# One batch at a time in a cached-attention decode block: V in 64 KB rows, K in two halves, one softmax per batch

## The chip, the cores and the metric

One core of one Trainium2 chip runs one launch. Times are microseconds of device time. A time quoted for a kernel is the median of its runs. For a core that runs alone, a run counts as slow when it lies more than 1.5% above the fastest of the same kernel; comparisons use the fast runs, and a kernel seen only once has no state ("unknown"). All ratios below are the mean time of one kernel's fast runs over that of the other's fast runs of the same rounds (the profiled run left out), so they are not quite the ratio of the medians that I quote.

## The reference, cut to what matters

A decode step for eight sequences. Each has one new token, 32 query heads of 128, four kv heads, and a cache of 8192 positions.

```python
q = (h @ wq).reshape(8, 1, 32, 128)                      # h: modulated layernorm of x
scores = einsum('bhqd,bhkd->bhqk', q, k) * 128 ** -0.5   # k, v: 8 query heads share a kv head
o = einsum('bhqk,bhkd->bhqd', softmax(scores), v)
x = x + ga * (o @ wo)
gate, up = h2 @ W_gate, h2 @ W_up                        # h2: modulated layernorm of the new x
x = x + gb * ((gate * (gate > 0) * up) @ W_down)
```

K and V are 16.8 MB per batch together, 134 MB of the 186 MB that the program reads. Every byte is used once, so the bytes set a floor.

## The kernel before: the parts that matter

The kernel works on a half batch m at a time (two kv heads, 64 partitions each). K and V arrive in four rotating slots of 32 KB a partition. K is transposed by the vector engine (DVE) in eight pieces; the tensor engine (PE) multiplies each with Q; a max per row, spread over partitions by a small matmul, gives the exponential's bias; the probabilities are transposed by DVE; PE multiplies them with V. The result of P·V is folded by DVE at the next half batch.

```python
for m in range(M):                                  # M = 16 half batches
    for nm, t in (("k", A_k_cache), ("v", A_v_cache)):
        load((nm, m), ...rearrange("g (p c) d -> (g p) (c d)", p=64), 2 * SLOT)   # 32 KB a partition
...
for m in range(M):
    P.trip = m // 2                                 # two half batches per turn of the hardware loop
    for e8 in range(8):
        kt_part(m, e8); qk_part(m, e8)              # DVE transpose, then four matmuls
        if e8 == 5: rowmax(m, 0)
    fold(m - 1, 0); fold(m - 1, 1)
    rowmax(m, 1); spread(m)
    fold(m - 1, 2); headmax(m); expo(m); fold(m - 1, 3)
    fold_pe(m - 1); keep(m - 1)
    p_turn(m)
    make_qpad(m + 2)
    pv(m)
```

A helper turns the list of operations into a loop with counted semaphores. For each instruction of a turn it works out how far a counter must have come. This part is the same in both kernels; remember the expression `need[t][at] - base[sem] - t * by`, where `need` is 0 when an instruction waits for nothing.

```python
base[sem] = last[0] - by          # what the counter stands at when the first turn begins
for at in range(len(trips[0])):   # each instruction of a turn
    v = max(need[t][at] - base[sem] - t * by for t in range(n))
    if v > top:
        limit[at][sem] = top = v  # this instruction waits for the counter to reach v
```

Of the kernel before, what the change touches and what calls it, by code (L numbers as in the profile page):

```python
# [6 lines left out]
dt = mybir.dt  # L7
ACT = mybir.ActivationFunctionType
# [255 lines left out]
def bass_adaLN_cond__gqa_block_cached__glu_gated_reglu__decode_kernel(nc, A_x, A_k_cache, A_v_cache, A_wq, A_wo, B_x, B_W_gate, B_W_up, B_W_down, c, w_mod, out):  # L264
# [11 lines left out]
    SLOT = 8192  # L276
    RING = 16 * 4096
# [13 lines left out]
    with ExitStack() as es:  # L291
# [9 lines left out]
        ktb = sb("kt", [128, NKT * 2048], dt.bfloat16)  # L301
# [5 lines left out]
        jm = sb("jm", [128, 2, J], dt.float32)  # L307
        jms = sb("jms", [128, 2 * J], dt.float32)
        jmp = sb("jmp", [128, 2, J], dt.float32)
        im = sb("im", [128, 4], dt.float32)  # L310
# [10 lines left out]
        M = N // 2  # L321
        qR = sb("qR", [128, 4, M, J], dt.bfloat16)
        rq = sb("rq", [128, 2, 128], dt.bfloat16)
        mq = sb("mq", [128, 4], dt.bfloat16)
        qpad = sb("qpad", [128, 2, 4, 152], dt.bfloat16)
        prb = sb("prb", [128, 1024], dt.bfloat16)
        pT = sb("pT", [128, 2, 32, 2, 32], dt.bfloat16)
        negm = sb("negm", [128, 4], dt.float32)
        mj = sb("mj", [128, 2 * J], dt.float32)
        mjt = sb("mjt", [128, 2 * J], dt.float32)  # L330
        bias = sb("bias", [128, 2], dt.float32)
        lall = sb("lall", [128, M], dt.float32)
        lx = sb("lx", [128, M, 2 * J], dt.float32)
        om = sb("om", [128, Dh], dt.float32)
        oacc = sb("oacc", [128, M + 1, 2 * J], dt.float32)
# [21 lines left out]
        for t in "kv":  # L357
            for i in range(2):
                sems[(t, i)] = E(nc.semaphore("%s_%d" % (t, i)))

        def at(m):

            return m if P.turn is None else 2 * P.turn + m % 2
# [12 lines left out]
        stream, place, cursor = [], {}, [0]  # L376

        def load(key, src, n):
            stream.append((key, src, n))

        def pump():
            while stream:
                key, src, n = stream[0]
                lo = cursor[0] if cursor[0] + n <= RING else 0
                if P.unread("arena", lo, lo + n):
                    return
                stream.pop(0)
                cursor[0] = lo + n
                place[key] = lo
                dst = arena[:, lo:lo + n]  # L390
                if len(src.shape) == 3:
                    dst = dst.rearrange("p (a n) -> p a n", a=src.shape[1])
                P.op("sp", lambda e, dst=dst, src=src: e.dma_start(dst, src), writes=[slot_r(lo, lo + n)], dma=True,
                     own=(key[0], key[1] % 2) if key[0] in "kv" else None)
                if key[0] in "kv":
                    P.held[key] = (lo, lo + n)
# [7 lines left out]
        load(("wm", 0), wm_src[:, 0:D], D)  # L404
        load(("wm0", 0), wm_src[:, D:24 * D], 23 * D)
        load(("wm", 1), wm_src[:, 24 * D:48 * D], 24 * D)
        for i in range(2):
            load(("wq", i), wq_src[:, 2 * i * SLOT:2 * (i + 1) * SLOT], 2 * SLOT)
        for m in range(M):
            for nm, t in (("k", A_k_cache), ("v", A_v_cache)):  # L410
                load((nm, m), t[m // 2, 2 * (m % 2):2 * (m % 2) + 2].rearrange("g (p c) d -> (g p) (c d)", p=64), 2 * SLOT)
        wo_parts = [(0, 16), (16, 32)]
        for i, (r0, r1) in enumerate(wo_parts):
            load(("wo", i), wo_src[:, r0 * D:r1 * D], (r1 - r0) * D)
        gu_parts = [(0, 4), (4, 8)]
        for i, (r0, r1) in enumerate(gu_parts):
            load(("gate", i), g_src[:, r0 * F:r1 * F], (r1 - r0) * F)
            load(("up", i), u_src[:, r0 * F:r1 * F], (r1 - r0) * F)
        wd_parts = [(0, 14), (14, 21), (21, 25), (25, 27), (27, 28)]
        for i, (r0, r1) in enumerate(wd_parts):  # L420
            load(("wd", i), d_src[:, r0 * D:r1 * D], (r1 - r0) * D)
# [10 lines left out]
        def aff(e, t, base, pat):  # L432
# [9 lines left out]
        P.op("pool", lambda e: e.memset(qpad[:], 0.0), writes=[R("qpad", 0, 2)])  # L442
        P.op("pool", lambda e: e.memset(pT[:], 0.0), writes=[R("pT", 0, 4)])
# [6 lines left out]
        P.op("pool", lambda e: e.tensor_copy(rq[:].rearrange("p t (h l x) -> p (t h) l x", h=2, l=2),  # L450
                                             identf[:].rearrange("p (q x) -> p q x", q=4)[:, :, None, :].to_broadcast([128, 4, 2, 32])),
             reads=[R("identf")], writes=[R("rq")])

# [21 lines left out]
        P.op("dve", lambda e: e.tensor_reduce(jm[:], identf[:].rearrange("p (g m j) -> p g j m", g=2, j=J), AX.X, ALU.add),  # L475
             reads=[R("identf")], writes=[R("jm")])
        P.op("dve", lambda e: e.tensor_reduce(jmp[:], identf[:].rearrange("p (t g i j) -> p g j t i", t=2, g=2, j=J), AX.XY,
                                              ALU.add), reads=[R("identf")], writes=[R("jmp")])
        P.op("dve", lambda e: e.tensor_reduce(im[:], identf[:].rearrange("p (t i j) -> p i t j", t=4, j=J), AX.XY, ALU.add),
# [58 lines left out]
        for i in range(2):  # L538
            fns = []
            for kk in range(4 * i, 4 * i + 4):  # L540
                w = arena[:, place["wq", i] + (kk % 4) * 4096:place["wq", i] + (kk % 4 + 1) * 4096].rearrange("p (g z n) -> p g z n", g=4, z=2)
                for z in range(2):
                    for g in range(4):
                        fns.append(lambda e, w=w, z=z, g=g, kk=kk: hold(e.matmul(  # L544
                            ps[32 * g:32 * g + 32, 3 + z, :], hT[:, kk, :], w[:, g, z, :],
                            start=(kk == 0), stop=(kk == KC - 1), tile_position=(0, 32 * g)), z > 0))
            P.op("pe", fns, reads=[R("hT"), slot_r(place["wq", i], place["wq", i] + 2 * SLOT)], writes=[bank(3, 2)])
        qs = ktb[:, 6144:7168].rearrange("p (i x) -> p i x", x=32)
        qT = ktb[:, 7168:8192].rearrange("p (i r) -> p i r", r=32)
        for z in range(2):  # L550
            src = ps[:, 3 + z, :].rearrange("p (u x r) -> p u r x", u=J, r=2)
            dst = qs[:, 16 * z:16 * z + 16, :].rearrange("p (u r) x -> p u r x", r=2)
            res, resT = ("kt", 6144 + 512 * z, 6656 + 512 * z), ("kt", 7168 + 512 * z, 7680 + 512 * z)
            if z == 0:
                P.op("dve", lambda e, s=src, d=dst: e.tensor_copy(d, s), reads=[bank(3 + z)], writes=[res])  # L555
            else:
                P.op("act", lambda e, s=src, d=dst: e.activation(d, s, ACT.Copy), reads=[bank(3 + z)], writes=[res])
# [5 lines left out]
        P.op("pe", [lambda e, t=t: e.matmul(ps[:, 5, 256 * t:256 * t + 256].rearrange("p (i b) -> p i b", b=B), rq[:, t, :],  # L563
                                            qT[:, :, 0:2 * B:2], start=True, stop=True) for t in range(2)],
             reads=[("kt", 7168, 8192), R("rq")], writes=[bank(5)])
        for u in range(4):
            src = ps[:, 5, :].rearrange("p (t j u b) -> p u b t j", t=2, j=J, u=4)[:, u]
            P.op("dve", lambda e, s=src, u=u: e.tensor_copy(qR[:, u].rearrange("p (b t) j -> p b t j", t=2), s),
                 reads=[bank(5)], writes=[R("qR", u, u + 1)])



        QE = SLOT // 4

        def make_qpad(m):
            if m >= M:
                return
            P.op("pool", lambda e: e.tensor_tensor(  # L578
                out=qpad[:, m % 2, :, 24:152].rearrange("p u (q c) -> p u q c", q=4)[:, :, :, 0:J],
                in0=qR[:, :, m, None, :].to_broadcast([128, 4, 4, J]), in1=mq[:, None, :, None].to_broadcast([128, 4, 4, J]),  # L580
                op=ALU.mult), reads=[R("qR", 0, 4), R("mq")], writes=[R("qpad", m % 2, m % 2 + 1)])

        def kt_part(m, e8):
            lo = place["k", m] + e8 * QE
            to = (8 * m + e8) % NKT * QE
            P.op("dve", lambda e: e.transpose(ktb[:, to:to + QE].bitcast(dt.uint32), arena[:, lo:lo + QE].bitcast(dt.uint32)),  # L586
                 reads=[slot_r(lo, lo + QE)], writes=[R("kt", to, to + QE)], own_wait=("k", m % 2) if e8 == 0 else None)

        def qk_part(m, e8):
            to = (8 * m + e8) % NKT * QE  # L590
            i = e8 % 4
            b = 2 * (m % 2) + e8 // 4
            kv = ktb[:, to:to + QE].rearrange("p (c t k r) -> p c t k r", t=2, k=32, r=2)
            fns = []
            for t in range(2):
                for r in range(2):
                    fns.append(lambda e, t=t, r=r: e.matmul(  # L597
                        ps[:, b, :].rearrange("p (c k) -> p c k", k=32), qpad[:, m % 2, t * 2 + r, 24 - 8 * i:152 - 8 * i],
                        kv[:, :, t, :, r], start=(i == 0 and t == 0 and r == 0), stop=(i == 3 and t == 1 and r == 1)))
            P.op("pe", fns, reads=[R("kt", to, to + QE), R("qpad", m % 2, m % 2 + 1)],  # L600
                 writes=[bank(b)])
# [237 lines left out]
```

## Time and profile before

| | before |
|---|---|
| median time | 436.93 us (436.91 to 437.25) |
| loads' queue busy | 98.9% of 16 DMA engines |
| read rate over the attention part | 433 GB/s |
| DVE busy | 265.8 us |
| PE busy | 277.4 us |

The following lines are from the page of the kernel before: span, busy times, the share of DMA in 40 equal slices (9 is 90% or more) with the rate below it, the load queue, the engines of the chain that ended last, and two of the costliest groups (busy us, mean ns of one; then idle time before it and what ended that). PEld are PE's weight loads, ACT is the scalar engine, POOL is GpSimd, SP issues the DMAs; a q behind a name (DVEq, SPq) means that engine's sequencer, which waits and issues. L181 is the line that waits for the landing of a K or V load.

```profile
span 435.6 us, 3869 instructions
...
PE 277.4 (64%) x1643; PEld 120.8 (28%) x1483; DVE 265.8 (61%) x377; ACT 29.9 (7%) x62; POOL 14.5 (3%) x32
...
PE   0415238659595958768595958768595958636437
...
DVE  1503058777686877777778777677788776253020
...
DMA  9999999999999999999999999999999999999995
GB/s 373 438 444 433 429 433 433 434 430 432 433 433 433 433 433 433 433 433 433 433 433 433 433 433 433 433 433 433 433 433 433 433 433 433 423 429 444 428 420 233
...
q1 hardware_dynamic: 6944, 185.61, 98.9%
...
PE 46%; DVE 20%; issue 13%; DMA 6%; ACT 0%; SPq 0%
...
L586 DVE STREAM_TRANSPOSE kt<-arena 128x1024 uint32<-128x1024 uint32 x128 | 149.6, 1217 | 39.0 <-PE ps L597 26.8
...
L636 DVE STREAM_TRANSPOSE pT<-prb 64x1024 bf16<-64x1024 bf16 x32 | 39.6, 1239 | 18.1 <-ACT prb L629 17.6
```

The windows view gives the attention part as one stretch (columns: busy us and count for each engine, granted PE clock, DMA share, rate):

```profile
core 0 of [0], span 435.6 us
...
52.00:373.00 321.00, 228.60 (x1090) 99.00 (x1074) 239.76 (x327) 22.32 (x50) 6.34 (x16) 0.83 1.00 433
```

DMA share 1.00 means that the 16 DMA engines together had no hole that shows. Yet the chain names PE and DVE. The timeline shows one half batch (start, duration, engine, line, operation, result and source, count, and in brackets the idle time before it):

```profile
211.19 0.69 DVE L609 TENSOR_REDUCE negm<-ps 128x1 f32<-128x512 f32 x1 [0.52 <-PE ps L597]
...
213.29 1.11 ACT L629 ACTIVATE prb<-ps,bias 128x1024 bf16<-128x1024 f32 x1 [18.75 <-DVE mjt L623]
...
214.52 2.51 DVE L636 STREAM_TRANSPOSE pT<-prb 64x1024 bf16<-64x1024 bf16 x2 [1.10 <-ACT prb L629]
...
217.13 6.58 PE L646 MATMUL ps<-arena,pT 128*64 128x512 bf16 x32 [3.26 <-issue]
217.22 4.62 DVE L586 STREAM_TRANSPOSE kt<-arena 128x1024 uint32<-128x1024 uint32 x4 [0.19 <-DVEq L181]
...
223.64 5.38 PE L597 MATMUL ps<-kt,qpad 128*128 128x512 bf16 x24
...
237.38 3.06 PE L646 MATMUL ps<-arena,pT 128*64 128x512 bf16 x14 [3.26 <-issue]
```

From one P·V group (217.13) to the next (237.38) is 20.25 us; over all 16 groups the mean is 19.59. The transfers of one half batch are 16 rows of 32 KB per DMA engine at 1213 ns each (from the DMA records of the trace), 19.4 us.

### The profile page before, as it was taken

Reading aid. Unit: us, or ns where it says so; the run is one execution under the profiler, and the core shown is the slowest. Engines: PE = TensorE matmul, PEld = TensorE weight load, DVE = VectorE, ACT = ScalarE, POOL = GpSimd, SP = SyncE. Lnnn points to the kernel's source line nnn. Section 1 sums busy time; section 2 is a strip of 40 time slices with the busy share of each in tenths; the row PEclk is TensorE's granted clock in tenths of the full one; section 3 lists DMA queues with packets and bytes.
Section 4 is the critical chain, followed back from the end, with each engine's and each line's share of the span. In section 5 each row is a group of like instructions: output and inputs, shape, how many; then the busy total and the mean of one; then the engine's idle time right before and its main releaser. Section 6 shows DMA issues by size and latency. Waiting matters only on the chain.

```text
span 435.6 us, 3869 instructions
## 1 busy us (share of the span) xinstructions
PE 277.4 (64%) x1643; PEld 120.8 (28%) x1483; DVE 265.8 (61%) x377; ACT 29.9 (7%) x62; POOL 14.5 (3%) x32
## 2 busy tenths in 40 slices
PE   0415238659595958768595958768595958636437
PEld 0100002324242423324242333324142323334105
DVE  1503058777686877777778777677788776253020
ACT  2000010110101010010101010010101010110000
POOL 7000000000000000000000000000000000000000
PEclk9966668697888869696978969696987969668858
DMA  9999999999999999999999999999999999999995
GB/s 373 438 444 433 429 433 433 434 430 432 433 433 433 433 433 433 433 433 433 433 433 433 433 433 433 433 433 433 433 433 433 433 433 433 423 429 444 428 420 233
DMA packets 7078, 185.74 MB, mean 426 GB/s; under 512 B 832, under 2 KB 928, under 8 KB 1312
## 3 DMA queue, kind: packets, MB, share of 16 engines
q1 hardware_dynamic: 6944, 185.61, 98.9%
q8 instruction: 5, 0.08, 0.1%
q10 hardware_dynamic: 128, 0.04, 0.0%
q14 instruction: 1, 0.01, 0.0%
HBM read 185.63 MB, written 0.02 MB: 426 GB/s over the span
## 4 chain that ended last, share of the span: by engine, by line
PE 46%; DVE 20%; issue 13%; DMA 6%; ACT 0%; SPq 0%
PE ps L646 22%; PE ps L597 18%; DVE kt L586 9%; DMA arena<-in_B_W_down_dram 6%; DVE negm L609 5%; PE ps L615 2%; PE ps L663 2%; PE ps L743 1%; DVE om L657 1%; DVE mj L620 1%; PE ps L774 1%; DVE mjt L623 1%; DVE negm L613 1%; DVE kt L733 0%; DVE lx L706 0%
## 5 line engine op out<-in xcount | busy, mean ns | idle before, releaser
L586 DVE STREAM_TRANSPOSE kt<-arena 128x1024 uint32<-128x1024 uint32 x128 | 149.6, 1217 | 39.0 <-PE ps L597 26.8
L597 PE MATMUL ps<-kt,qpad 128*128 128x512 bf16 x512 | 122.4, 385 | 9.6 <-DVE kt L586 8.3
L646 PE MATMUL ps<-arena,pT 128*64 128x512 bf16 x512 | 95.4, 554 | 51.7 <-issue 51.7
L646 PEld LDWEIGHTS ps<-arena,pT 128*64 128x64 bf16 x512 | 45.5, 157 | 95.5 <-issue 91.1
L597 PEld LDWEIGHTS ps<-kt,qpad 128*128 128x128 bf16 x512 | 46.0, 97 | 84.6 <-DVE kt L586 28.7
L636 DVE STREAM_TRANSPOSE pT<-prb 64x1024 bf16<-64x1024 bf16 x32 | 39.6, 1239 | 18.1 <-ACT prb L629 17.6
L629 ACT ACTIVATE prb<-ps,bias 128x1024 bf16<-128x1024 f32 x16 | 17.8, 1113 | 293.1 <-DVE mjt L623 293.1
L609 DVE TENSOR_REDUCE negm<-ps 128x1 f32<-128x512 f32 x32 | 22.1, 692 | 12.7 <-PE ps L597 12.7
L663 PE MATMUL ps<-jmp,om 128*128 128x16 f32 x34 | 7.4, 293 | 17.0 <-DVE om L657 17.0
L657 DVE SCALAR_TENSOR_TENSOR om<-ps,im,om 128x128 f32<-128x128 f32 x51 | 17.7, 347 | 0.7
L615 PE MATMUL ps<-identf,negm 128*128 128x128 f32 x32 | 7.8, 326 | 15.6 <-DVE negm L613 15.6
L578 POOL TENSOR_TENSOR qpad<-qR,mq 128x128 bf16<-128x128 bf16 x16 | 6.3, 399 | 317.6 <-DVE pT L636 267.7
L774 PE MATMUL ps<-arena,hT 128*32 128x448 bf16 x128 | 9.4, 459 | 9.4 <-DMA arena<-in_B_W_up_dram 6.8
L544 PE MATMUL ps<-arena,hT 128*32 128x512 bf16 x64 | 7.1, 623 | 12.7 <-DMA arena<-in_A_wq_dram 12.7
L521 PE MATMUL ps<-arena,hT 128*32 128x512 bf16 x96 | 9.2, 565 | 9.2 <-DMA arena<-in_w_mod_dram 9.2
L793 PE MATMUL ps<-arena,hmT 128*32 128x256 bf16 x112 | 8.7, 320 | 5.6 <-DMA arena<-in_B_W_down_dram 5.4
L528 DVE COPY mod<-ps 128x512 f32<-128x512 f32 x2 | 1.3, 671 | 17.8 <-PE ps L521 17.8
L781 DVE TENSOR_TENSOR kt<-ps,kt 128x448 bf16<-128x448 f32 x2 | 1.2, 621 | 17.6 <-PE ps L774 17.6
L663 PEld LDWEIGHTS ps<-jmp,om 128*128 128x128 f32 x34 | 5.7, 210 | 20.5 <-DVE om L657 20.5
L615 PEld LDWEIGHTS ps<-identf,negm 128*128 128x128 f32 x32 | 4.7, 187 | 23.6 <-DVE negm L613 23.6
L555 DVE CAST kt<-ps 128x512 bf16<-128x512 f32 x1 | 0.7, 692 | 16.3 <-PE ps L544 16.3
L793 PEld LDWEIGHTS ps<-arena,hmT 128*32 128x32 bf16 x112 | 6.2, 114 | 9.0 <-DMA arena<-in_B_W_down_dram 7.6
(89 smaller groups left out, 89.2 us busy)
## 6 DMA issues: line engine op xcount, KB each, us to landing
arena<-in_A_k_cache_dram SPq DMA_DIRECT2D x16, 4096.0 KB, 21.1
arena<-in_A_v_cache_dram SPq DMA_DIRECT2D x16, 4096.0 KB, 19.0
arena<-in_A_wq_dram SPq DMA_DIRECT2D x2, 4096.0 KB, 34.9
arena<-in_A_wo_dram SPq DMA_DIRECT2D x2, 4096.0 KB, 18.0
arena<-in_B_W_gate_dram SPq DMA_DIRECT2D x2, 3584.0 KB, 15.5
arena<-in_B_W_up_dram SPq DMA_DIRECT2D x2, 3584.0 KB, 19.0
arena<-in_w_mod_dram SPq DMA_DIRECT2D x1, 6144.0 KB, 30.7
arena<-in_w_mod_dram SPq DMA_DIRECT2D x1, 5888.0 KB, 16.6
```

The lines of the kernel that those rows point to most:

```text
L521: fns.append(lambda e, w=w, pr=pr, j=j, kk=kk: hold(e.matmul(ps[32 * j:32 * j + 32, pr, :], hT[:, kk, :], w[:, 2 * pr:2 * pr + 2, j, :], s ...
L586: P.op("dve", lambda e: e.transpose(ktb[:, to:to + QE].bitcast(dt.uint32), arena[:, lo:lo + QE].bitcast(dt.uint32)), reads=[slot_r(lo, lo ...
L597: fns.append(lambda e, t=t, r=r: e.matmul(ps[:, b, :].rearrange("p (c k) -> p c k", k=32), qpad[:, m % 2, t * 2 + r, 24 - 8 * i:152 - 8 * ...
L609: P.op("dve", lambda e: e.tensor_reduce(negm[:, h:h + 1], ps[:, b, :], AX.X, ALU.max, negate=True), reads=[bank(b)] + (free(("v", m - 1)) ...
L615: P.op("pe", lambda e: e.matmul(ps[:, 4, 0:128], negm[:, 2:3].to_broadcast([128, 128]), identf[:], start=True, stop=True), reads=[R("negm" ...
L629: P.op("act", lambda e: e.activation(prb[:], ps[:, 2 * z:2 * z + 2, :].rearrange("p h n -> p (h n)"), ACT.Exp, bias=bias[:, z:z + 1], scal ...
L636: P.op("dve", lambda e, g=g: e.transpose(pT[64 * g:64 * g + 64, z, :, g, :], prb[64 * g:64 * g + 64, :]), reads=[R("prb")] + ([R("qpad", z ...
L646: fns.append(lambda e, t=t: e.matmul(ps[64 * (t % 2):64 * (t % 2) + 64, 5, :].rearrange("p (i d) -> p i d", d=Dh), pT[:, z, t].rearrange(" ...
L657: P.op("dve", lambda e, i=i: e.scalar_tensor_tensor(out=om[:], in0=ps[:, 5, Dh * i:Dh * i + Dh], scalar=im[:, i:i + 1], in1=om[:], op0=ALU ...
L663: P.op("pe", lambda e: e.matmul(ps[:, 6 + z, 0:16], om[:], jmp[:].rearrange("p g j -> p (g j)"), start=True, stop=True), reads=[R("om"), R ...
L774: fns.append(lambda e, w=w, r=kk - r0, kk=kk, h=h, j=j, b0=b0: hold(e.matmul(ps[32 * j:32 * j + 32, b0 + h, 0:H], hT[:, kk, :], w[:, r, j, ...
L793: fns.append(lambda e, w=w, r=k - r0, k=k, i2=i2, j=j: e.matmul(ps[32 * j:32 * j + 32, 4, 0:256], hmT[:, k, 1 - i2:33 - i2], w[:, r, i2, j ...
```

## The change

Intent: a whole batch per turn, a kv head on each quadrant of 32 partitions, so that V of all four heads is one DMA with 64 KB a partition, K comes in two halves of 32 KB, and the max, exponential and fold chain is paid once per batch. wo, gate and up come whole, too. The cost is that V has one buffer, not two.

```diff
-        for m in range(M):
-            for nm, t in (("k", A_k_cache), ("v", A_v_cache)):
-                load((nm, m), t[...].rearrange("g (p c) d -> (g p) (c d)", p=64), 2 * SLOT)
+        for b in range(B):
+            k = A_k_cache[b].rearrange("g (p c) d -> (g p) (c d)", p=32)
+            load(("ka", b), k[:, 0:HALF], HALF, HALF)
+            load(("kb", b), k[:, HALF:SLOT], HALF, 0)
+            load(("v", b), A_v_cache[b].rearrange("g (p c) d -> (g p) (c d)", p=32), SLOT, VPART)
+        load(("wo", 0), wo_src, KO * D, 0)
+        load(("gate", 0), g_src, KC * F, VPART)
+        load(("up", 0), u_src, KC * F, 0)
 ... (layout constants, masks and tensors cut)
+        def p_turn(b, f):       # one transpose, then a masked copy per kv head
+            P.op("dve", lambda e: e.transpose(pd[:, f], prb[:, f]), ...)
+            for g in range(G):
+                P.op("dve", lambda e, g=g: e.tensor_scalar(out=pT[:, f, :, :, g, :], in0=pd[:, f]...,
+                                                           scalar1=mqf[:, g:g + 1], ..., op0=ALU.mult), ...)
+        def fold(b):            # two multiplies; the first frees V
+            ... reads=[bank(5), R("im")] + (free(("v", b)) if i == 0 else [])
 ... (Q·K and P·V index arithmetic cut: P·V is now 128 matmuls of 256 columns, was 64 of 512)
+        for b in range(B):
+            P.trip = b
+            for e in range(16):
+                kt_part(b, e)
+                qk_part(b, e)
+                if e == 1:
+                    fold(b - 1)
+                if e == 2:
+                    fold_pe(); keep(b - 1)
+                if e in (8, 10, 15):
+                    rowmax(b, {8: 0, 10: 1, 15: 2}[e])
+            rowmax(b, 3)
+            headmax(b)
+            for f in range(2):
+                expo(b, f)
+            for f in range(2):
+                p_turn(b, f)
+                if f == 0:
+                    make_qpad(b + 1)
+                pv(b, f)
```

(Lines shortened in the third and fourth hunk.)

## The prediction

> **What bounds the kernel now.** The DMA queues. The page shows 98.9% busy on the queue that carries the loads; the slices read 428 to 444 GB/s in the attention part without a dip, and the program moves 185.74 MB. The Trainium skill ("DMA: Bandwidth & Descriptors", section "Bandwidth") puts the ceiling of the path into SBUF at 435 GB/s; this trace agrees with 433 over 52 to 373 us. The DMA records are busy 430.9 us per DMA engine of a 435.6 us span: about 1 us of start and 3.6 us of tail are not transfer. The chain of waits names PE (46%) and DVE (20%) because their loop is nearly as long: P·V groups start 19.6 us apart, and a pair of 4 MB loads takes 19.4 us. Engine work is not the limit, but has no room.
>
> **Transfers.** Bytes stay. A 48 KB row takes 1815 ns, a 32 KB row 1213, a 28 KB row 1062: 36.7 ps a byte plus about 9 ns a row. V and wo as 64 KB rows and gate/up as 56 KB rows remove 88 rows per DMA engine; 19 fewer DMAs remove 19 completion writes of 9 ns. Estimate: 0.8 + 0.2 = 1.0 us less; 0.3 us if a 64 KB row is cut in two.
>
> **Engines, per batch (estimates from this trace).** K transposes stay at 16 x 1.16 us, Q·K at 64 matmuls, row maxima at four of 0.69. The max chain (1.4 us from row max to exponential) runs once, before twice. The P transposes become two of 1.24 us and eight masked copies (bf16, 1024 columns): about 0.35 us each at four elements a cycle, as the skill ("VectorE: DVE Perf Modes", section "The perf-mode tier table") states for this kind; 1.1 us at one. No run yet shows which. Folds shrink from eight to two. P·V streams the same columns in twice the matmuls: 8.4 to 10 us with the slow clock that this trace has at its start.
> Loop from one P·V end to the next: fold 0.7 + fourteen transposes 16.2 + row maxima and last Q·K 3.0 + max chain 1.4 + exp 1.2 + transpose and masks 3.0 + P·V 9.3 = 35 us, below the 38.8 us that a batch's bytes need (38.5 with slow masks).
>
> **The new danger.** V has one 64 KB buffer. The next V is issued only after P·V and the fold, which sits behind two K transposes. Counted from a V landing: P·V ends at +9.3, the next first K half lands at +9.7, the fold is done at +12.7, bytes start near +14.5; the queue holds 19.4 us of K. Slack about 5 us, 1 to 2 with slow masks. The tail has slack too: all of up now waits for its last row (1.9 us more work), but hidden states are ready 2.2 us before the first down part lands.
>
> **Time.** Only the transfers are critical: 436.95 - 0.8 = **436.1 us**, 8 in 10 within 435.2 to 438.5. Faster by over 2%: 1%; within 2%: 93%; slower by over 2%: 6%.
>
> **What would show it.** Slices still at 433 to 436 GB/s, no dip each batch; V issued well before the second K half lands; 65536-byte rows of about 2417 ns; DVE busy time down, with idle time waiting for K loads; tail unchanged.
>
> **What would make it wrong.** Masked copies at one element per cycle plus P·V cold throughout (13.6 us): loop about 42 us, DMA gaps of 3 us a batch, 455 to 465 us. Or large rows that transfer slower.

## The result, and the profile after

The changed kernel takes 436.51 us (median of four runs, 436.38 to 436.69) against 436.93. The ratio is 0.9989, with a 95% interval of 0.9972 to 1.0006: the same.

The same lines of its page:

```profile
span 435.1 us, 4774 instructions
...
PE 259.8 (60%) x2139; PEld 136.1 (31%) x1979; DVE 249.3 (57%) x342; ACT 29.5 (7%) x54; POOL 8.8 (2%) x22
...
DMA  9999999999999999999999999999999999899995
GB/s 374 425 458 434 429 434 434 477 387 473 401 428 434 476 398 428 434 476 392 434 440 470 392 434 440 431 431 476 398 428 434 476 398 470 386 429 481 393 416 232
...
q1 hardware_dynamic: 5360, 185.61, 98.9%
...
DMA 12%; PE 4%; DVE 1%; SPq 0%; issue 0%
...
L576 DVE STREAM_TRANSPOSE kt<-arena 128x1024 uint32<-128x1024 uint32 x128 | 148.5, 1213 | 61.2 <-DVEq L181 44.6
...
L626 PE MATMUL ps<-arena,pT 128*64 128x256 bf16 x1024 | 72.5, 315 | 51.4 <-PEq L181 51.4
...
L616 DVE TENSOR_SCALAR pT<-pd,mqf 128x1024 bf16<-128x1024 bf16 x64 | 28.2, 503 | 0.6
```

```profile
core 0 of [0], span 435.1 us
...
52.00:373.00 321.00, 216.43 (x1618) 117.68 (x1602) 226.96 (x296) 21.88 (x42) 4.87 (x8) 0.88 1.00 434
```

What the reader should see. DVE is busy 16.5 us less (265.8 to 249.3), PE 17.6 us less (277.4 to 259.8), and the time is 0.4 us less. The DMA row is still 9 everywhere and the attention part still has share 1.00 at 434 GB/s. The chain that ended last names DMA 12% and PE 4%, where it was PE 46% and DVE 20%; but these shares add up to 17% of the span, since the chain could be followed back only to 362 us, so it tells of the tail and not of the attention part. There the idle times before the groups show the change: the K transposes waited 44.6 us for landings of K (DVEq L181) and P·V 51.4 us for landings of V (PEq L181).

The single slices of the rate swing from 386 to 481 GB/s although the windows view finds no hole. A V row of 64 KB lasts 2418 ns in the DMA records, and a slice is 10.9 us, so if whole rows are counted where they start, a slice gains or loses up to two tenths. The windows view of two neighbours at 477 and 387 GB/s (76.13 to 87.01 and 87.01 to 97.89 us) says so: it gives them DMA shares of 1.10 and 0.90, and a share over 1 is no real load. With rows this long, neither the rate nor the share of so short a stretch proves a stall; the share over the long attention part shows that there was none.

One batch in the timeline of the changed kernel:

```profile
207.28 9.13 PE L626 MATMUL ps<-arena,pT 128*64 128x256 bf16 x128 [6.47 <-PEq L181]
216.97 2.37 DVE L576 STREAM_TRANSPOSE kt<-arena 128x1024 uint32<-128x1024 uint32 x2 [8.22 <-DVEq L181]
...
219.26 0.57 DVE L635 TENSOR_SCALAR om<-ps,im 128x128 f32<-128x128 f32 x2
...
219.60 0.33 SPq L391 DMA_DIRECT2D arena<-in_A_v_cache_dram  x1
...
228.45 9.40 SPq L391 DMA_DIRECT2D arena<-in_A_k_cache_dram  x2
...
238.06 0.69 DVE L592 TENSOR_REDUCE negm<-ps 128x1 f32<-128x512 f32 x1 [0.56 <-PE ps L586]
...
240.17 1.11 ACT L608 ACTIVATE prb<-ps,bias 128x1024 bf16<-128x1024 f32 x1 [17.40 <-DVE mjt L603]
...
245.76 1.67 DVE L616 TENSOR_SCALAR pT<-pd,mqf 128x1024 bf16<-128x1024 bf16 x4
...
245.92 6.30 PE L626 MATMUL ps<-arena,pT 128*64 128x256 bf16 x86 [6.43 <-PEq L181]
```

P·V at 207.28 starts when V has landed (its last row ends at 206.80 in the DMA records), 9.13 us. The first transpose, which had waited for the first K half, starts at 216.97, a second follows, the fold at 219.26 frees V, and V is issued at 219.60. Its first bytes move at 224.28, so the issue was 4.7 us early. The next P·V starts at 245.92, 38.64 us later; the mean over the eight groups is 38.68. The transfers of a batch are 8 rows at 2418 and 16 at 1213 ns per DMA engine: 38.75 us. So the loads set the pace.

### The profile page after: what moved, and what is told of

It reads as the page before. It is cut to its first block, busy times and chain, and to the rows that moved or that the text cites. A ratio compares the mean times of both kernels' runs of the same rounds, so it can differ in the third digit from the quotient of the medians.

```text
span 435.1 us, 4774 instructions
## 1 busy us (share of the span) xinstructions
PE 259.8 (60%) x2139; PEld 136.1 (31%) x1979; DVE 249.3 (57%) x342; ACT 29.5 (7%) x54; POOL 8.8 (2%) x22
## 5 line engine op out<-in xcount | busy, mean ns | idle before, releaser
L576 DVE STREAM_TRANSPOSE kt<-arena 128x1024 uint32<-128x1024 uint32 x128 | 148.5, 1213 | 61.2 <-DVEq L181 44.6
L586 PE MATMUL ps<-kt,qpad 128*128 128x512 bf16 x512 | 134.2, 385 | 43.0 <-DVE kt L576 37.2
L626 PE MATMUL ps<-arena,pT 128*64 128x256 bf16 x1024 | 72.5, 315 | 51.4 <-PEq L181 51.4
L626 PEld LDWEIGHTS ps<-arena,pT 128*64 128x64 bf16 x1024 | 70.1, 129 | 53.2 <-issue 52.7
L586 PEld LDWEIGHTS ps<-kt,qpad 128*128 128x128 bf16 x512 | 40.8, 99 | 132.5 <-DVE kt L576 98.9
L616 DVE TENSOR_SCALAR pT<-pd,mqf 128x1024 bf16<-128x1024 bf16 x64 | 28.2, 503 | 0.6
L614 DVE STREAM_TRANSPOSE pd<-prb 128x1024 bf16<-128x1024 bf16 x16 | 19.8, 1239 | 10.9 <-ACT prb L608 10.9
L645 ACT ACTIVATE oacc<-ps 128x32 f32 (+1 forms) x9 | 1.8, 198 | 157.7 <-PE ps L640 157.7
L744 PEld LDWEIGHTS ps<-arena,hT 128*32 128x32 bf16 x64 | 2.3, 137 | 26.5 <-DMA arena<-in_B_W_up_dram 12.3
L714 PE MATMUL ps<-arena,kt 128*32 128x256 bf16 x128 | 5.7, 362 | 5.1 <-DMA arena<-in_A_wo_dram 5.1
L598 PE MATMUL ps<-identf,negm 128*128 128x128 f32 x16 | 3.9, 326 | 7.8 <-DVE negm L596 7.8
## 6 DMA issues: line engine op xcount, KB each, us to landing
arena<-in_w_mod_dram SPq DMA_DIRECT2D x1, 5888.0 KB, 16.5
```

Source lines behind the costliest of these rows:

```text
L576: P.op("dve", lambda e_: e_.transpose(ktb[:, to:to + PART].bitcast(dt.uint32), arena[:, lo:lo + PART].bitcast(dt.uint32)), reads=[slot_r(l ...
L586: fns.append(lambda e_, t=t, r=r: e_.matmul(ps[:, e // 4, :].rearrange("p (c k) -> p c k", k=32), qpad[:, t * 2 + r, 24 - 8 * i:152 - 8 * ...
L614: P.op("dve", lambda e: e.transpose(pd[:, f], prb[:, f]), reads=[R("prb", f, f + 1)], writes=[R("pd", 1024 * f, 1024 * f + 1024)])
L616: P.op("dve", lambda e, g=g: e.tensor_scalar(out=pT[:, f, :, :, g, :], in0=pd[:, f].rearrange("p (c i x) -> p c i x", c=32, i=2), scalar1= ...
L626: fns.append(lambda e, n=n, h=h, c_=c_, i=i, t=t: e.matmul(ps[64 * t:64 * t + 64, 5, 0:2 * Dh].rearrange("p (i d) -> p i d", d=Dh), pT[:, ...
L714: fns.append(lambda e, w=w, k=k, j=j: e.matmul(ps[32 * j:32 * j + 32, 5, 0:256], oX[:, k, :], w[:, k, j, :], start=(k == 0), stop=(k == KO ...
```

## The experiments

**Theory.** The loads alone set the time of both kernels. The change shortens the engine loop from about 39.2 us a batch to about 36, but the loads hide that; the 0.4 us comes from fewer rows. **Rivals.** (a) The single V buffer or the softmax chain keeps the new engine loop as tight as the old, so there is no hidden gain. (b) The 0.4 us comes from the engines, not from the rows.

### The same added work in both kernels

The last row maximum is computed again n times; each repeat waits for the one before it, so the work lies on the chain from the last Q·K to the exponential and the result stays the same.

```diff
+        def again(n, b, h):
+            for _ in range(n):
+                P.op("dve", lambda e: e.tensor_reduce(negm[:, h:h + 1], ps[:, b, :], AX.X, ALU.max, negate=True),
+                     reads=[bank(b), R("negm", h, h + 1)], writes=[R("negm", h, h + 1)])
             rowmax(b, 3)
+            again(4, 3, 3)      # 12 in the larger dose; before: again(2, ..., 1) per half batch
             headmax(b)
```

> The kernel before with its second row maximum computed two times more in each half batch (0.65 us each on DVE, on the chain from last Q·K to exponential): 1.3 us more per half batch, 2.6 per batch. My theory: the engine loop of the kernel before (19.6 us per half batch) already equals its transfers (19.4 us), so nearly all of the added work shows: 16 x 1.3 = 20 us, less a few us of lead in the queue, so 452 to 459 us, with DMA gaps. Rival (the loads alone bind, the engine loop has spare time in both kernels): within 1 us of 437.

Measured: 449.74 us, ratio 1.0296 (1.0279 to 1.0313). The kernel before has no room, as the theory says, but the size missed: P·V groups are 20.51 us apart on average (19.59 without the work), so 0.9 us of the added work shows per half batch, because the P·V groups themselves became shorter (5.39 us on average, 5.96 before; more on this in the last section).

> The changed kernel with the same 2.6 us of added DVE work per batch (its last row maximum four times more). My theory: its engine loop is about 36 us against 38.8 us of transfers, so the work vanishes: 436.3 to 438 us, no DMA gap. Rival (the loop is as tight as before): 20 us more, about 456.

Measured: fast runs of 448.1 to 454.0 us, ratio 1.0345 (1.0276 to 1.0413). My theory of the headroom fails here. The changed kernel is slowed by the same work about as much as the kernel before. How much is less sure than the interval says: the profiled run (455.1 us, slow) lost 8 us before the second batch's V (its first row starts at 116.3 us, at 108.2 in the changed kernel), with rows of 48 KB at 2036 ns against 1815, and the two runs at 453.7 and 454.0 us lie so near it that they may have lost the same. The one run that most likely did not, 448.1 us, is 11 us above the kernel before, whose own added work cost 13.

> The changed kernel with 12 more row maxima per batch, 7.8 us. My theory: headroom of about 3 us is used up, so the batch becomes 36 + 7.8 = 44 us, 5 us over the transfers, times 7 to 8 batches: 468 to 478 us. The headroom is 7.8 us less the growth per batch. If the loop had far more room than I think (masks and P·V overlap more): below 450.

Measured: 489.8 to 491.3 us in the three fast runs of five, ratio 1.122. Outside my range. In the trace (of a slow run) the P·V groups are 46.14 us apart on average.

### The loads taken away

Only a quarter of each K and V piece is loaded from the second batch on, so the spacing of the P·V groups is the engine loop itself. The attention is wrong; the comparison with the reference still passed, so it is not sensitive to this, and nothing below rests on it.

```diff
-                dst = arena[:, lo:lo + n]
+                cut = n // 4 if key[0] in ("ka", "kb", "v") and key[1] > 0 else n
+                dst, src = arena[:, lo:lo + cut], src[:, 0:cut]
```

> The changed kernel, but from the second batch on each K half and each V brings only a quarter of its bytes (wrong result on purpose; the rest of the buffer is read as it was). The loads no longer bind, so the spacing of the P·V groups is the engine loop itself. My theory: 35 to 37 us per batch, below 38.8. Rival (the engine loop is as long as the transfers): 38.5 us or more.

> The kernel before, with a quarter of the bytes of every K and V from the third half batch on (wrong result on purpose). The spacing of the P·V groups is then the engine loop itself. My theory: 19.6 us per half batch as in the normal run (39.2 per batch), so the engines, not only the loads, were at their limit. Rival (the spacing of 19.6 us followed the loads): clearly below 19.4, such as 18.

Measured (one look each, state unknown; I use only the spacing). The kernel before: 19.74 us per half batch, but this includes a first spacing of 21.68, before which the loads were still whole; without it 19.60, 39.2 per batch, as in the normal run. With the loads out of the way nothing got shorter, so its engines were at their limit by themselves. The changed kernel: 37.42 us per batch, not 35 or 36. So the changed kernel has 38.7 - 37.4 = 1.3 us of room, not 3.7, and four repeats at 0.72 us (2.87 us in the trace of that run) overrun it: 37.4 + 2.9 = 40.3, and 40.30 us is what the trace of the four-repeat kernel shows (a slow run, but its slow rows came before the first P·V; the spacings scatter from 39.2 to 40.9).

Where the missing 2.4 us are is in the timeline of the changed kernel with the light loads:

```profile
203.40 9.91 PE L627 MATMUL ps<-arena,pT 128*64 128x256 bf16 x128 [5.13 <-DVE pT L617]
204.53 1.68 DVE L617 TENSOR_SCALAR pT<-pd,mqf 128x1024 bf16<-128x1024 bf16 x4
213.35 2.37 DVE L577 STREAM_TRANSPOSE kt<-arena 128x1024 uint32<-128x1024 uint32 x2 [7.15 <-PE ps L627]
...
215.65 0.57 DVE L636 TENSOR_SCALAR om<-ps,im 128x128 f32<-128x128 f32 x2
...
240.90 9.28 PE L627 MATMUL ps<-arena,pT 128*64 128x256 bf16 x116 [5.13 <-DVE pT L617]
```

The second set of masked copies ends at 206.21. The first K half had been in place for long, and yet the first transpose starts at 213.35, right after P·V (203.40 + 9.91 = 213.31), and the releaser named is PE's P·V. My sum had the first two transposes beside P·V. Nothing in the data requires this wait: the K transpose writes a buffer that the Q·K matmuls of the previous batch have long read. It comes from the helper's expression. In the loop of the changed kernel the counter of PE for DVE starts at base -1 (the first turn's fold must not wait for a P·V that never was, so the counter is raised by one ahead of the loop). For the first instruction of the first turn, which needs nothing, the expression gives 0 - (-1) - 0 = 1, and 1 is above 0, so "wait for 1" is placed there. From the second turn on, 1 means that P·V of the previous batch is finished. The fold, two transposes later, then finds its wait already made. In the loop of the kernel before, no such wait stands on the first transpose (there the base of this counter is 0).

### The wait moved to where it belongs

```diff
-                v = max(need[t][at] - base[sem] - t * by for t in range(n))
+                v = max([need[t][at] - base[sem] - t * by for t in range(n) if need[t][at]], default=0)
```

The instructions stay the same and in the same order; only the wait moves from the first transpose to the fold (printing the helper's waits while both kernels are built shows no other difference).

> The same moved wait in the kernel with a quarter of the K and V bytes (wrong result on purpose). P·V groups were 37.4 us apart; my theory says 35.1 us now, which is the loop that the prediction summed. Rival (another term of the sum was wrong): stays above 36.5.

Measured: 34.10 us per batch, below what I expected. The timeline shows the two transposes beside P·V, and the fold waiting for it:

```profile
202.40 8.80 PE L627 MATMUL ps<-arena,pT 128*64 128x256 bf16 x128 [5.13 <-DVE pT L617]
203.53 1.67 DVE L617 TENSOR_SCALAR pT<-pd,mqf 128x1024 bf16<-128x1024 bf16 x4
205.12 2.36 DVE L577 STREAM_TRANSPOSE kt<-arena 128x1024 uint32<-128x1024 uint32 x2
...
211.24 0.61 DVE L636 TENSOR_SCALAR om<-ps,im 128x128 f32<-128x128 f32 x2 [3.76 <-PE ps L627]
...
236.53 3.67 PE L627 MATMUL ps<-arena,pT 128*64 128x256 bf16 x34 [5.13 <-DVE pT L617]
```

Compared with the same view above: the transposes start at 205.12, inside P·V (202.40 to 211.20), and the fold starts at 211.24. That is worth the 2.3 us between the first transpose and the fold above (213.35 to 215.65). The other 1.1 us is P·V itself, 8.80 us here and 9.91 there. The clock records of the traces say why: here 3.36 us of P·V ran at half clock, there 5.64, and half of the 2.28 us between them is 1.1 us.

> The same moved wait in the kernel with four more row maxima per batch (2.9 us by its trace), which without it ran at 40.3 us a batch and 448 to 454 us. My theory: 35.1 + 2.9 = 38.0 us, below the 38.7 of the loads, so the added work vanishes: 436.3 to 437.5 us. Rival (the wait is not the cause): above 446 us as before.

Measured: 437.06 us (three fast runs, 436.5 to 437.6, and a slow one of 444.9), ratio 0.9993 (0.9975 to 1.0010) to the kernel before. The added work that cost at least 11 us without this edit costs nothing that shows with it: that the misplaced wait took the room is shown. The waits view (who waited for whom: us in total, times, longest) has the K transposes wait for P·V in the first kernel, and no longer for P·V but for their own sequencer's wait, the landing of K, in the second:

```profile
DVE kt L576 <- PE ps L631: 48.0, 7, 7.3
```

```profile
DVE kt L576 <- DVEq L181: 39.1, 8, 5.3
```

> The changed kernel with one wait moved: the loop's counter code put the wait for the last P·V on the first K transpose of a batch (an unneeded place; only the fold needs it). Now the fold waits, as the dependence asks, and two transposes may run beside P·V. My theory: the engine loop gets 2.3 us shorter (37.4 to 35.1), which the loads hide: 436.5 us, the same within 0.3. Rival (the shortened loop is worth something, because it, not the loads, sets the pace): faster than 436.0.

Measured: median 436.76 us with one slow run of 444.83 and one of 441.31 that counts as fast; ratio 1.0016 (0.9982 to 1.0051), the same. In the normal kernel P·V and the landing of the first K half end at almost the same time: the timeline above has P·V end at 216.41 and the transpose start at 216.97, and by the waits of that kernel (idle time before the K transposes: us, times) the landing came last in six batches and P·V in two:

```profile
  DVEq L181: 44.6, 6
  PE ps L626: 16.4, 2
```

So the misplaced wait cost next to nothing there. The room that the edit buys is real (the row above), and worth nothing as long as the loads set the time.

### How much slack the single V buffer has

The fold was moved behind the fifth and the eighth K transpose, which delays the issue of V.

```diff
-                if e == 1:
+                if e == 4:          # 7 in the second
                     fold(b - 1)
-                if e == 2:
+                if e == 5:          # 8
                     fold_pe()
```

> The changed kernel with the fold of the previous batch after the fifth K transpose instead of the second: V is issued 3 x 1.16 = 3.5 us later. The trace has V issued 6.2 us before its first bytes move[...]: slack 4.3 us. My theory: no DMA gap, 436.4 to 437.2 us. Rival (the single V buffer has no slack): 7 x 3.5 = 25 us more.

Measured: 441.93 us (one of four runs slow), ratio 1.0102 (1.0081 to 1.0122). Missed: five us, 0.7 us per batch (P·V groups 39.37 us apart, 38.68 without). The 6.2 us of the expectation are not in the DMA records: V is issued 4.65 to 4.73 us before its first row.

> The fold after the eighth K transpose: V issued 7.0 us later, 2.7 us more than the slack. My theory: a DMA gap of about 2.7 us before each of the seven V loads that wait for a fold, so 436.5 + 19 = 455 us (450 to 460). Rival (the row of loads can catch up, or the slack is larger): under 445.

Measured: 454.52 us, ratio 1.0400, and P·V groups 41.00 us apart. The time is as expected, but not by the hole of 2.7 us that I gave for it, as the next lines show. The timeline and the windows view show the fold behind eight transposes, the late issue, and the hole in the DMA:

```profile
224.13 9.13 DVE L576 STREAM_TRANSPOSE kt<-arena 128x1024 uint32<-128x1024 uint32 x8 [10.47 <-DVEq L181]
...
233.18 0.57 DVE L635 TENSOR_SCALAR om<-ps,im 128x128 f32<-128x128 f32 x2
...
233.51 0.33 SPq L391 DMA_DIRECT2D arena<-in_A_v_cache_dram  x1
```

```profile
229.00:234.40 5.40, 5.02 (x20) 1.41 (x18) 5.36 (x7) 0.00 (x0) 0.00 (x0) 1.00 0.68 291
234.40:270.00 35.60, 22.32 (x180) 13.82 (x181) 22.49 (x31) 2.50 (x5) 0.63 (x1) 0.86 1.01 428
```

DMA share is 0.68 in the 5.4 us up to the first V bytes, a loss of 1.7 us there by this view; with the records cut at the edges of the stretch it is 1.3, and from one V issue to the next the 16 DMA engines stand idle for 1.5 us on average. V rows slower than 2418 ns add 0.7 us a batch, and these two make up nearly all of the 2.3 us by which the spacing grew. With the queue dry, the first V row starts 0.94 to 0.96 us after the issue in all seven batches. So the slack of the changed kernel is its 4.7 us of lead less about 0.95, some 3.7 us; I had predicted 5. The term that was too large is the K in the queue, 19.4 us: from the last row of a V to the first of the next only 17.5 us pass (206.80 to 224.28), because the DMA engines do not finish together (the eight rows of V per engine, 19.3 us of rows, lie between 185.60 and 206.80). The smaller delay of 3.4 us should then just have fitted, and did not quite: leads of 0.95 to 1.71 us remained there, V rows took up to 4148 ns against 2418, and a batch lost 0.7 us. Why rows are slow with so little queued behind them I did not settle.

### The row count undone

V goes back to two DMAs with 32 KB a partition each, with a semaphore each; in the second kernel also wo, gate and up go back to two each.

```diff
-            load(("v", b), ..., SLOT, VPART)
+            load(("va", b), v[:, 0:HALF], HALF, VPART)
+            load(("vb", b), v[:, HALF:SLOT], HALF, VPART + HALF)
```

> Only V in two DMAs of 32 KB a partition; wo, gate, up whole. 64 rows more per DMA engine at 8 ns each: records 0.5 us busier, 436.9 us. P·V of the first half can start 9.7 us earlier, so the V issue comes earlier too; my theory says that this is worth nothing. Rival: faster than the changed kernel.

> The changed kernel with its rows cut back: V in two DMAs of 32 KB a partition, wo, gate and up in two each, everything else as changed. My theory: the 0.4 us of the change is the row count alone, so the busy time of the records per DMA engine goes from 430.2 back to 430.9 us and the time to 436.9 to 437.1. Rival (the gain came from the shorter engine work): stays at 436.5.

Measured: 436.65 us (ratio 0.9997, 0.9983 to 1.0010) with V alone undone, 437.04 us (ratio 1.0005, 0.9992 to 1.0019) with all undone. The busy time of the records per DMA engine is exact enough to tell them apart: 430.87 us before, 430.18 changed, 430.69 with V in halves, 430.87 with all undone. The sums come back to the second decimal. The times follow in the same order, but their intervals overlap, so that the 0.4 us in the time is the rows is supported, not proved, by the times alone. What speaks against rival (b) is the second kernel: it has all of the new engine work, and its five runs (436.84 to 437.28 us) do not keep the gain (436.38 to 436.69 in the changed kernel, measured in other rounds). V in two DMAs says less: by its trace P·V started only 1.5 us earlier (205.82 against 207.28), as it then waited for the probabilities, and V was issued no earlier (219.54 against 219.60), as the first transpose still waited for K. My expectation of an earlier issue missed.

## Why the prediction was right, and the step of it that was wrong

- **The loads bound the kernel, and still do.** Right. DMA share 1.00 before and after; P·V groups 38.68 us apart against 38.75 us of rows.
- **"Engine work is not the limit, but has no room"** before. Right, shown twice: 2 x 19.60 us with light loads, and 13 us lost to added work. It understated a little: the loop alone (39.2 us) is longer than the loads (38.8).
- **Rows.** The price of a row was right: 2418 ns for 65536 bytes (predicted 2417). The trace's total fell by 0.69 us; I had estimated 1.0 and used 0.8. The time fell by 0.42. Inside the range.
- **Masked copies** at four elements a cycle: right in kind. Four of them take 1.67 or 1.88 us, 0.42 to 0.47 each (predicted 0.35); 1024 elements at one per 0.96 GHz cycle, the clock that the Trainium skill ("VectorE: DVE Perf Modes", section "Specifications") gives, would by estimate be 1.07 us, and at two per cycle 0.53.
- **P·V** per batch: 8.57 to 9.71 us, predicted 8.4 to 10. Right.
- **The engine loop of 35 us** is the step that failed. "fourteen transposes" after the fold assumes that the first two run beside P·V. They did not, because the loop helper put the wait for P·V on the first transpose. The loop is 37.4 us; the term that was mis-sized is two transposes, 2.3 us, that measured as fully exposed. Moving the wait gives 34.1 us. The time was still right since either value lies below 38.8, in part by luck: the margin that the argument counted on was 3.8 us, and 1.3 were there.
- **The slack of V, 5 us**: measured 3.7 by the issue's lead, and a delay of 3.4 us already costs 0.7 us a batch. It was over-estimated, with no effect on the time.
- **The tail**: right, but with less to spare. The whole up product takes 5.35 us after its landing (3.18 before, for a half), and the hidden states are ready at 423.50 us, 0.15 us before the down product starts (421.75 before, 2.28 us ahead). The down product itself starts at 423.65 (424.03 before), and the final store is issued at 433.46 of 435.1 us (433.96 of 435.6 before), so the tail is unchanged.
- **"Slices still at 433 to 436 GB/s"** was wrong as a sign, as told above.

## What to carry to other kernels

When loads fill every slice, shorter engine work buys only room, and only a dose of added work or taking the loads away shows how much room there is (here 1.3 us a batch; with one wait moved, 4.6). Sum a loop by what each instruction is made to wait for in the built program, not by what the data need, since generated synchronization can place a wait earlier than the dependence. A single large buffer in the place of two smaller ones is safe as long as its refill is issued before the queue of the others runs out, and that margin can be read from issue to first byte.

No version here beats both kernels by more than noise. The bytes at the measured row times take 430 of the 435 us span, and the runs offer no way to read fewer.

## What the Trainium skill lacked or had wrong

- "DMA: Bandwidth & Descriptors", section "Bandwidth", has the ceiling (435 GB/s; the attention part reads 433 to 434) but no cost of a large row issued by SyncE (its 10.5 ns a packet is for a 4 KB load issued from GpSimd). The records give about 9 ns a row beside 36.7 ps a byte: 1213 ns for 32 KB, 2418 ns for 64 KB, 432.2 and 433.7 GB/s over 16 engines. A row of 64 KB is one record, not cut.
- The same page, section "Latency and other measured facts", gives about 600 ns to the first byte for such an issue. Here, with the queue dry, 0.94 to 0.96 us passed from the start of the issue to the first row in seven of seven cases. The issuing instruction itself takes 0.33 us of that; counted from its end, 0.61 to 0.63 us pass and the page agrees. What it lacks is where the 600 ns begin.
- "TensorE: Matmul & The Clock Gate", section "Part 1: The HAM clock gate (the "warmup" mystery)", says that the window of 3413 ns runs freely. The clock records of the traces agree: in each of the eight that I looked at, all changes of PE's granted clock lie whole multiples of 3.413 us apart. What I found on no page: a loop paced by the engines seems to settle on whole multiples of it. With the added work the kernel before settles at 20.47 to 20.49 us per half batch (6 windows are 20.48), the changed one with light loads at 37.50 to 37.53 (11 are 37.54), with the wait moved at 34.12 to 34.14 (10 are 34.13), and the unchanged kernel before repeats 18.68, 19.57, 20.02, 20.25, together 78.52 (23 are 78.50). P·V starts on the slow clock each time (in all groups of these traces), and its length depends on when the clock rises; with the moved wait and light loads the records show 6.83 us of half clock and 27.31 of full seven times in a row, together 34.13. That this holds the loop at a multiple is my reading; I made no run to test it. It matters for experiments: 1.4 us of added work per half batch showed as 0.9, and the moved wait as 3.3 where 2.3 was its own.
